# Transposes of tile 2's keys and queries by transfers instead of TensorE, with the work around them dealt anew

## The chip, the cores and the metric

The kernel runs on one core of one Trainium2 chip. A core has TensorE (PE; its weight loads are shown apart as PEld), VectorE (DVE), ScalarE (ACT), GpSimd (POOL) and SyncE (SP), and 16 DMA engines that serve the queues of all of them. The metric is the device time of one execution in microseconds.

## The reference

Windowed attention over q, k and v of shape (batch 8, heads 8, sequence 576, head size 64), then a two-layer network with a quick GELU over its 4608 rows of 512.

```python
# attention, window = 32
scores = scale * np.matmul(q, k.transpose(0, 1, 3, 2))
mask = np.abs(pos[:, None] - pos[None, :]) <= window
scores = np.where(mask, scores, -1000000000.0)
...
attn = attn / (np.sum(attn, axis=-1, keepdims=True) + 1e-09)
np.matmul(attn, v)
...
# x: (4608, 512), w_in: (512, 2048), w_out: (2048, 512)
h = x @ w_in
g = h * (1.0 / (1.0 + np.exp(-1.702 * h)))
return (g @ w_out).astype(np.float32)
```

## The kernel before

The 4608 rows are cut into 36 units of 128 and nine tiles of four units (512 rows); the rows of queries are shifted by 32 against those of keys. The order of all instructions is written out by hand. On each engine they run in that order, and each waits for the semaphores of what it needs.

**Attention of a unit.** `load_kq(c, u)` has GpSimd's queue bring the keys or queries of unit `u`, cast to bf16, into a staging buffer (`kst` or `qst`, five of each). They must be transposed, so that the head size lies on the partitions: `kT` and `qT`, seven buffers of each. `T_dma(c, u)` does that by a transposing transfer on SyncE's queue (L240); `turn(u)` is `T_dma("q", u)` and `T_dma("k", u + 1)`. `T_pe(which, eng)` does it on TensorE: three tensors at a time, four 128x128 transposes each, into PSUM (L249), and one copy each from PSUM by the engine named. `scores(u, tag)` multiplies keys and queries in 24 small products and takes the exponential on ScalarE (L284); it needs the queries of `u` and the keys of `u` and `u + 1`. `band(u)` masks on VectorE (L314), `values(u, tag)` multiplies with the values, `norm(u)` divides on VectorE (L344, L345). `x_T` and `x_T2` transpose the result for one or two units into `xT`. The values come by `load_v(u)` on GpSimd's queue, and GpSimd copies them to an odd offset with `odd_v(u)` (L227). `fetch(u)` is the loads of `q` of `u`, `k` of `u + 1` and `v` of `u + 1`; `ahead("kq", u)` leaves the values out.

**The two layers.** Both use a scheme of seven products on halves of the matrices in place of eight. It needs sums of weights (`w1_sums`, `w2_sums`), of inputs (`x_sums`) and of activations (`g_sums`; `g0_sum` for tile 0), all on VectorE. `l1_group(t, n, fill, side)` is a quarter of layer one of tile `t`: seven products into four PSUM banks, two copies on ScalarE and two additions on VectorE (L537, L543) between them, four GELUs on ScalarE (L524). Between its products, `fill(1)`, `fill(7)`, `fill(2)` and `fill(4)` put in pieces of layer two of the tile before, and `side(0)` and `side(1)` sums on VectorE. Layer two is one list of pieces, `l2`, of one product each; `do(l2, n)` issues the next `n`. Its first 32 pieces (`layer2_plain`) are one part of tile 0 without the scheme; the copies of the results out of PSUM go with certain pieces, on the engine that `l2eng` or `seed2` names at that point. Stores go on SyncE's queue.

**Where the change lies.** `opening` computes the attention of tiles 0 and 1 and layer one of tile 0. `first_layer1` is layer one of tile 1 with layer two of tile 0 between: four groups, `n` from 0 to 3. In each, two odd-offset copies and the loads `fetch(12 + n)` are issued on GpSimd. In groups 1 to 3, after product 7's fill, `T_pe` transposes the keys and queries of tile 2's units 8 to 11 (and 12's keys) on TensorE; in group 3, `turn(12)` and `turn(13)` send units 12 and 13 to SyncE. Then `run` computes the attention of units 8 to 15 with layer two between: units 8 to 11 are tile 2's, 12 to 15 tile 3's. From `back(2)`, layer one of tile 2, on, every tile goes the same way: `front` and `back`, with its transposes by `T_dma`.

Of the kernel before, what the change touches and what calls it, by code (L numbers as in the profile page):

```python
# [16 lines left out]
BF16 = mybir.dt.bfloat16  # L17
F16 = mybir.dt.float16
I32 = mybir.dt.int32
AF = mybir.ActivationFunctionType  # L20
ALU = mybir.AluOpType

SQ = 64
# [3 lines left out]
class _Kernel:  # L27
# [201 lines left out]


    def place(self, c, u):
        t = self.sb(c + "T", [128, 4, 128], BF16, 7)
        (self.kT if c == "k" else self.qT)[u] = t
        return t

    def T_dma(self, c, u):
# [1 line left out]
            return  # L238
        src = self.stage.pop((c, u))
        self.nc.sync.dma_start_transpose(self.place(c, u), src.rearrange("p h d -> p (h d)"))  # L240

    def T_pe(self, which, eng):

        tp = self.bank("t", [128, 4, 4, 128], BF16, "tp")
        which = [(x[0], int(x[1:])) for x in which]
        for i, (c, u) in enumerate(which):
            src = self.stage.pop((c, u)).rearrange("p h d -> p (h d)")
            for hp in range(4):
                self.nc.tensor.transpose(tp[:, i, hp, :], src[:, 128 * hp:128 * hp + 128], self.ident)  # L249
        for i, x in enumerate(which):  # L250
            self.copy(eng, self.place(*x), tp[:, i])

# [9 lines left out]
            self.sc.setdefault(u, []).append(x)  # L264
            self.mm(x, self.ident, self.bias, start=True)

    def scores(self, u, tag):
        kT, q = self.kT[u], self.qT[u]
        nxt = self.k_first if u == self.NU - 1 else self.kT[u + 1][:, :, 0:64]
        sc = self.score_banks(tag)  # L270
        for hp in range(4):
            c = 128 * hp
            start = hp == 0
            for eo in range(2):
                r = slice(64 * eo, 64 * eo + 64)
                lo, hi = sc[eo][0:64], sc[eo][64:128]
                self.mm(lo[:, c:c + 64], kT[r, hp, 0:64], q[r, hp, 0:64], start=start)
                self.mm(hi[:, c:c + 128], kT[r, hp, 64:128], q[r, hp, :], start=start)
                self.mm(lo[:, c + 64:c + 128], nxt[r, hp, :], q[r, hp, 64:128], start=False)
        if u % 2 == 0:  # L280
            self.pp = self.sb("p", [128, 2, 2, 8, SQ], BF16, 2)
        p = self.p[u] = self.pp[:, u % 2]
        for eo in range(2):
            self.nc.scalar.activation(p[:, eo].rearrange("k h s -> k (h s)"), sc[eo], AF.Exp, scale=self.scale)  # L284

    def scores_pair(self, u):

# [15 lines left out]
        for x in range(2):  # L303
            for eo in range(2):
                self.nc.scalar.activation(p[:, eo, x].rearrange("k h b s -> k (h b s)"), sc[2 * x + eo], AF.Exp,
                                          scale=self.scale)

    def band(self, u, eng=None):
        p = self.p[u]
        cross = [(2 * u + i) % 9 == 8 for i in range(2)]  # L310
        a, b = 0 if cross[0] else 1, 2 if cross[1] else 3
        pv = p.rearrange("p e (h b) s -> p (e h) b s", b=2)
        msk = self.mask[:, a:b + 1:b - a, :].rearrange("p (o b) s -> p o b s", o=1)
        (eng or self.nc.vector).tensor_mul(pv, pv, msk.to_broadcast([128, 8, 2, SQ]))  # L314

# [38 lines left out]
    def values_four(self, u):  # L354

        D = self.D
        p = [self.p.pop(u + i) for i in range(4)]
        b = {tag: self.bank(tag, name="pv") for tag in "AECt"}
        self.acc[u] = b | {"t0": b["t"][:, 0], "t1": b["t"][:, 1]}
        for tag in self.FOUR:  # L360
            lo, n, pad = self.four(tag)
            for i in range(n):
                x, h = divmod(lo + i, self.H)
                at, more = pad + i * (D + 1), pad * (i == 0)
                for blk in range(2):
                    vt = (self.ve[(u + x) % 9], self.odd(u + x))[blk].rearrange("p h d -> p (h d)")
                    self.mm(self.acc[u][tag][64 * blk:64 * blk + 64, at - more:at + D + 1],
                            p[x][:, h % 2, h // 2 * 2 + blk, :], vt[:, h * (D + 2) - more:h * (D + 2) + D + 1],
                            start=(i == 0))

    def norm_four(self, u, tags, units):
# [197 lines left out]
    def layer2_plain(self, t, pr):  # L569

        st = {}

        def part(i, f):
            if not st:
                st.update({j: self.bank("L" + "AB"[j], name="o") for j in range(2)})
                st["o"] = self.sb("o_sb", [128, 2, self.DM], F32, 2)
            lo = 256 * i + 128 * pr
            self.mm(st[i], self.g[t][:, f, lo:lo + 128], self.w2[:, f, :], start=(f == 0))
            if f == 15:
                self.copy((self.nc.vector, self.nc.scalar)[i * pr], st["o"][:, i, :], st[i])  # L580
                if i == 1:
                    self.store(t, pr, st["o"])

        return [lambda i=i, f=f: part(i, f) for q in range(8) for i in range(2) for f in (2 * q, 2 * q + 1)]
# [230 lines left out]
    @staticmethod  # L815
    def do(fs, n=99):
        for _ in range(min(n, len(fs))):
            fs.pop(0)()
# [76 lines left out]
    def run(self):  # L895
        pool, act = self.nc.gpsimd, self.nc.scalar
        self.l2eng = self.seed2 = act
        more = self.l2 = self.layer2_plain(0, 0) + self.layer2([(i, j) for i in range(self.NT) for j in range(2)][1:-1],
                                                               (self.NT - 1, 1))
        self.opening()  # L900
        self.do(self.x_sums(1))
        late = self.first_layer1()
        do = self.do
        dve = self.nc.vector
        self.scores(8, "t")
        self.scores(9, "AC")
        self.turn(14)
        self.turn(15)
        do(late)
        do(more, 20)  # L910
        self.scores(10, "BE")
        do(more, 12)
        self.l2eng = dve
        self.band(8)
        self.band(9)
        do(more, 4)
        self.values(8, "t")
        self.values(9, "AC")
        self.odd_v(12, pool)
        self.odd_v(13, pool)  # L920
        self.scores(11, "BE")
        self.norm(8)
        self.band(10)
        self.norm(9)
        do(more, 8)
        self.scores(12, "t")
        do(more, 4)
        self.values(10, "AC")
        self.norm(10)
        self.band(11)  # L930
        self.scores(13, "BE")
        do(more, 8)
        self.x_T2(8, "t", act)
        self.values(11, "AC")
        self.norm(11)
        self.scores(14, "BE")
        do(more, 4)
        self.x_T(10, "A", dve)
        do(more, 2)
        self.x_T(11, "C", dve)  # L940
        self.scores(15, "t")
        do(more, 2)
        do(self.x_sums(2))
        self.seed2 = dve
        self.odd_v(14, pool)
        self.odd_v(15, pool)
        self.ahead("kq", 16)
        late = self.back(2)
        for t in range(3, self.NT):
            self.front(t, late)  # L950
            late = self.back(t)
        self.l2eng = act
        self.do(late, 2)
        self.do(self.l2, 16)
        self.do(late)
        self.do(self.l2, 999)

    def first_layer1(self):

        def b(*which):  # L960
            return [lambda i=i, j=j: self.w2_sums((i,), j) for i, j in which]

        dv = b((3, 0), (3, 1), (1, 0), (1, 1))
        extra = {0: [lambda: self.w1_sums((4,), 1), lambda: self.g0_sum(1)] + b((2, 0), (2, 1)), 1: b((4, 0), (4, 1)),
                 2: [lambda: self.g0_sum(2)], 3: []}
        for n in range(4):
            if n == 3:
                self.turn(12)
                self.turn(13)
            self.odd_v(8 + n, self.nc.gpsimd)  # L970
            self.fetch(12 + n)

            def fill(i):
                self.do(self.l2, dict(zip((1, 7, 2, 4), ((1, 1, 3, 3), (1, 1, 3, 5), (2, 2, 8, 4), (2, 2, 6, 6))[n]))[i])
                self.do(dv, {1: 2, 7: 1, 2: 0, 4: 2}[i] if n else {1: 0, 7: 1, 2: 0, 4: 1}[i])
                if i == 7 and n:
                    self.T_pe([("k8", "q8", "k9"), ("q9", "k10", "q10"), ("k11", "q11", "k12")][n - 1], self.nc.scalar)

            self.l1_group(1, n, fill, lambda i: self.do(dv, 1))
            dv += self.g_sums(1, 2 * n, 2) + extra[n]  # L980
        return dv

# [45 lines left out]
```

## Time and profile before

| | us |
|---|---|
| median of 3 runs (279.33 to 280.86) | 279.39 |
| the profiled execution | 279.59 |
| its span | 277.8 |
| layer one of tile 1 begins (first product after 43) | 43.47 |
| first scores of unit 8 | 65.31 |
| last scores ahead of tile 2's layer one (unit 15) | 77.78 |
| layer one of tile 2 begins | 78.39 |

Times inside the execution count from the start of the span. The profile is of one execution. A row of the timeline gives start and length in us, the engine, the line, the operation, out<-in by the program's names, the shape, and how many were merged; in brackets, idle time before it and what ended it. The names are `sc` for scores, `pv` for values, `tp` for transposes in PSUM, `h` for layer one, `o` for layer two, `g` and `gs` for activations and their sums, `a` and `b` for sums of weights. Matmuls are pipelined, so the length of a row is longer than its share of the time; the spacing of starts is the measure. A row of DMA issues ends with the time from issue to landing. SPq is SyncE's queue.

### The profile page before, as it was taken

Reading aid. Unit: us, or ns where it says so; the run is one execution under the profiler, and the core shown is the slowest. Engines: PE = TensorE matmul, PEld = TensorE weight load, DVE = VectorE, ACT = ScalarE, POOL = GpSimd, SP = SyncE. Lnnn points to the kernel's source line nnn. Section 1 sums busy time; section 2 is a strip of 40 time slices with the busy share of each in tenths; the row PEclk is TensorE's granted clock in tenths of the full one; section 3 lists DMA queues with packets and bytes.
Section 4 is the critical chain, followed back from the end, with each engine's and each line's share of the span. In section 5 each row is a group of like instructions: output and inputs, shape, how many; then the busy total and the mean of one; then the engine's idle time right before and its main releaser. Section 6 shows DMA issues by size and latency. Waiting matters only on the chain.

```text
span 277.8 us, 8904 instructions
## 1 busy us (share of the span) xinstructions
PE 266.3 (96%) x3652; PEld 224.8 (81%) x3652; DVE 212.1 (76%) x487; ACT 197.3 (71%) x346; POOL 138.6 (50%) x216
## 2 busy tenths in 40 slices
PE   1989999999999999999999999999999999999994
PEld 1668656888888888888888888888888888888883
DVE  3455898897899788878888887888798878855631
ACT  2586896989896689568966895698569856577420
POOL 8895597999592089729641974294430000000000
PEclk9999999999999999999999999999999999999999
DMA  8999999999999999999999999999992024202033
GB/s 86 166 206 195 178 207 168 170 150 164 139 162 189 155 121 153 174 176 166 188 178 153 130 172 148 163 145 139 136 136 77 2 82 74 76 2 76 2 113 117
DMA packets 150809, 37.74 MB, mean 136 GB/s; under 512 B 138608, under 2 KB 146416, under 8 KB 150768
## 3 DMA queue, kind: packets, MB, share of 16 engines
q0 software_dynamic: 106656, 18.42, 96.4%
q1 hardware_dynamic: 43664, 18.23, 38.0%
q8 instruction: 28, 0.46, 0.7%
q10 hardware_dynamic: 448, 0.52, 0.6%
q14 instruction: 13, 0.11, 0.1%
HBM read 36.83 MB, written 9.44 MB: 167 GB/s over the span
## 4 chain that ended last, share of the span: by engine, by line
PE 91%; DVE 4%; ACT 2%; issue 1%; POOL 1%; POOLq 0%; DVEq 0%
PE o L70 40%; PE h L70 39%; PE sc L70 5%; PE pv L70 4%; PE tp L179 1%; PE tp L203 1%; POOL kq L154 1%; ACT p L284 1%; DVE xn L345 1%; PE tp L409 0%; PE tp L249 0%; DVE b L433 0%; DVE o_sb L67 0%; PE tp L397 0%; ACT kq L67 0%
## 5 line engine op out<-in xcount | busy, mean ns | idle before, releaser
L524 ACT ACTIVATE g<-h 128x512 f16<-128x512 f32 x128 | 72.2, 599 | 37.9 <-PE h L70 31.6
L70 PEld LDWEIGHTS <-g 128*128 128x128 f16 x568 | 54.6, 98 | 8.1
L70 PE MATMUL h<-xs,a 128*128 128x256 f16 x384 | 57.6, 272 | 0.3 <-DVE h L537 0.3
L70 PEld LDWEIGHTS <-a 128*128 128x128 f16 x512 | 49.7, 97 | 8.8 <-issue 0.6
L70 PEld LDWEIGHTS <-w 128*128 128x128 f16 x496 | 47.6, 98 | 7.7
L70 PE MATMUL h<-xT,w 128*128 128x256 f16 (+1 forms) x368 | 53.6, 277 | 0.1
L70 PE MATMUL o<-w,g 128*128 128x256 f16 (+1 forms) x304 | 49.8, 284 | 0.0
L70 PEld LDWEIGHTS <-gs 128*128 128x128 f16 x416 | 39.7, 98 | 5.5 <-issue 0.2
L227 POOL COPY vo<-ve 64x264 int32<-64x264 int32 x71 | 35.1, 494 | 16.4 <-DMA ve<-in_v_dram 10.0
L70 PE MATMUL o<-b,gs 128*128 128x256 f16 x280 | 43.3, 273 | 0.0
L70 PE MATMUL o<-b,g 128*128 128x256 f16 x264 | 38.5, 273 | 0.0
L213 POOL DMA_DIRECT2D ve<-in_v_dram x40 | 34.1, 860 | 5.4 <-DMA w<-in_moe_w_out_dram 1.8
L537 DVE TENSOR_TENSOR h<-h,s 128x512 f32<-128x512 f32 x32 | 22.3, 698 | 18.3 <-PE h L70 18.2
L284 ACT ACTIVATE p<-sc 128x512 bf16<-128x512 f32 x64 | 32.6, 619 | 1.1 <-PE sc L70 1.0
L143 POOL DMA_DIRECT2D qst<-in_q_dram x35 | 28.2, 807 | 1.7 <-issue 1.6
L543 DVE TENSOR_TENSOR h<-h,s 128x512 f32<-128x512 f32 x32 | 22.3, 698 | 7.6 <-PE h L70 7.4
L143 POOL DMA_DIRECT2D kst<-in_k_dram x31 | 26.4, 854 | 0.6 <-DMA qst<-in_q_dram 0.4
L67 ACT COPY h<-h 128x512 f32<-128x512 f32 x32 | 18.8, 589 | 10.4 <-PE h L70 9.8
L886 POOL COPY seen<-gs 1x1 f16<-1x1 f16 x17 | 3.3, 196 | 39.3 <-DVE gs L456 39.3
L314 DVE TENSOR_TENSOR p<-p,mask 128x1024 bf16<-128x1024 bf16 x32 | 21.8, 699 | 0.7 <-ACT p L284 0.7
L67 ACT COPY o_sb<-o 128x256 f32<-128x256 f32 (+1 forms) x24 | 11.1, 462 | 12.8 <-PE o L70 12.8
L67 ACT COPY s<-h 128x512 f32<-128x512 f32 x32 | 19.2, 600 | 0.8
(94 smaller groups left out, 377.8 us busy)
## 6 DMA issues: line engine op xcount, KB each, us to landing
out_dram<-o_sb SPq DMA_DIRECT2D x33, 256.0 KB, 3.8
ve<-in_v_dram POOLq DMA_DIRECT2D x32, 128.0 KB, 6.3
kst<-in_k_dram POOLq DMA_DIRECT2D x25, 128.0 KB, 6.0
qst<-in_q_dram POOLq DMA_DIRECT2D x21, 128.0 KB, 5.7
w<-in_moe_w_out_dram POOLq DMA_DIRECT2D x4, 512.0 KB, 11.1
w<-in_moe_w_in_dram POOLq DMA_DIRECT2D x3, 512.0 KB, 9.3
qst<-in_q_dram POOLq DMA_DIRECT2D x7, 96.0 KB, 6.0
kq<-in_q_dram POOLq DMA_DIRECT2D x2, 256.0 KB, 6.0
```

The lines of the kernel that those rows point to most:

```text
L67: (eng.copy if eng is self.nc.scalar else eng.tensor_copy)(out, in_)
L70: self.nc.tensor.matmul(out, lhsT, rhs, start=start, stop=stop, skip_group_check=True)
L143: self.nc.gpsimd.dma_start(t[off:off + n], src[b, :, s:s + n, :].rearrange("h s d -> s h d"))
L154: self.nc.gpsimd.dma_start(self.stage["first"][0:n // j, :, at:at + j], src[0, :, lo:lo + n, :].rearrange("h (p j) d -> p h j d", j=j))
L213: self.nc.gpsimd.dma_start(t[off:off + n, :, :self.D], self.v[b, :, s:s + n, :].rearrange("h s d -> s h d"))
L227: eng.tensor_copy(*((words(vo[64:128]), words(self.ve[u % 9][64:128])), (words(vo[0:64]), words(nxt)))[i])
L284: self.nc.scalar.activation(p[:, eo].rearrange("k h s -> k (h s)"), sc[eo], AF.Exp, scale=self.scale)
L314: (eng or self.nc.vector).tensor_mul(pv, pv, msk.to_broadcast([128, 8, 2, SQ]))
L524: act.activation(g[:, f, 256 * half:256 * half + 256], bank.rearrange("p (i n) -> p i n", i=2), AF.Gelu_apprx_sigmoid)
L537: dve.tensor_add(e, b, s7)
L543: dve.tensor_add(c, b, s7)
L886: self.nc.gpsimd.tensor_copy(self.seen, self.gs[t - (n == 0)][0:1, 2, c, 255:256])
```

## The change

- `T_pe` is gone. In `first_layer1` the nine tensors that it transposed are issued by `T_dma` on SyncE's queue, three in each of groups 0 to 2; group 3 issues those of units 12 and 13, as before.
- The values of units 14 to 16 are loaded in group 3, after the keys and queries; before, one each in groups 1 to 3.
- The numbers of layer-two pieces and of sums in each gap of the four groups are new (`chunks`, `sums`): 56 pieces in place of 50. `w1_sums((4,), 1)` comes after the sums of group 0.
- The queries of units 12 and 13 lie side by side in one buffer, and their scores are one run of 40 products (`scores_two`). Scores of unit 10 come right behind those of 8 and 9, the second of its exponentials held back. Units 10 and 11 are transposed together by `x_T2`.
- `layer2_plain` copies both results on ScalarE, and `l2eng` is ScalarE in place of VectorE between units 8 and 15.

TensorE's order from layer one of tile 2 on is the same in both.

```diff
     def place(self, c, u):
+        if c == "q" and u in (12, 13):
+            if u % 2 == 0:
+                self.qT[u] = self.sb("q_two", [128, 4, 256], BF16, 1)
+            return self.qT[u - u % 2][:, :, 128 * (u % 2):128 * (u % 2) + 128]
...
-    def T_pe(self, which, eng):
-
-        tp = self.bank("t", [128, 4, 4, 128], BF16, "tp")
-        which = [(x[0], int(x[1:])) for x in which]
-        for i, (c, u) in enumerate(which):
-            src = self.stage.pop((c, u)).rearrange("p h d -> p (h d)")
-            for hp in range(4):
-                self.nc.tensor.transpose(tp[:, i, hp, :], src[:, 128 * hp:128 * hp + 128], self.ident)
-        for i, x in enumerate(which):
-            self.copy(eng, self.place(*x), tp[:, i])
...
+    def scores_two(self, u, tags):
+
+        k, q = [self.kT[u + i] for i in range(3)], self.qT[u]
+        sc = [x for tag in tags for x in self.score_banks(tag)]
+        for hp in range(4):
+            c = 256 * (hp % 2)
+            for eo in range(2):
+                r = slice(64 * eo, 64 * eo + 64)
+                for i in range(5):
+                    lo, hi = max(0, 64 * (i - 1)), min(256, 64 * (i + 1))
+                    rows = slice(64 * (i % 2), 64 * (i % 2) + 64)
+                    self.mm(sc[2 * (hp // 2) + eo][rows, c + lo:c + hi], k[i // 2][r, hp, rows], q[r, hp, lo:hi],
+                            start=c == 0 and i < 2)
...
             if f == 15:
-                self.copy((self.nc.vector, self.nc.scalar)[i * pr], st["o"][:, i, :], st[i])
+                self.copy(self.nc.scalar, st["o"][:, i, :], st[i])
...
         dve = self.nc.vector
+        do(more, 3)
         self.scores(8, "t")
         self.scores(9, "AC")
+        exps = self.scores(10, "BE", True)
         self.turn(14)
         self.turn(15)
         do(late)
-        do(more, 20)
-        self.scores(10, "BE")
-        do(more, 12)
-        self.l2eng = dve
+        do(more, 3)
         self.band(8)
         self.band(9)
-        do(more, 4)
+        self.l2eng = act
+        do(more, 16)
+        do(exps)
+        do(more, 8)
         self.values(8, "t")
         self.values(9, "AC")
...
-        do(more, 8)
-        self.scores(12, "t")
-        do(more, 4)
+        do(more, 12)
+        self.scores_two(12, ("t", "BE"))
         self.values(10, "AC")
+        self.band(11)
         self.norm(10)
-        self.band(11)
-        self.scores(13, "BE")
...
-        do(more, 4)
-        self.x_T(10, "A", dve)
-        do(more, 2)
-        self.x_T(11, "C", dve)
+        do(more, 6)
+        self.x_T2(10, "A", dve)
...
-        extra = {0: [lambda: self.w1_sums((4,), 1), lambda: self.g0_sum(1)] + b((2, 0), (2, 1)), 1: b((4, 0), (4, 1)),
+        extra = {0: [lambda: self.g0_sum(1)] + b((2, 0), (2, 1)) + [lambda: self.w1_sums((4,), 1)], 1: b((4, 0), (4, 1)),
                  2: [lambda: self.g0_sum(2)], 3: []}
         for n in range(4):
-            if n == 3:
-                self.turn(12)
-                self.turn(13)
+            for c, u in ((("k", 8), ("q", 8), ("k", 9)), (("q", 9), ("k", 10), ("q", 10)),
+                         (("k", 11), ("q", 11), ("k", 12)), (("q", 12), ("k", 13), ("q", 13), ("k", 14)))[n]:
+                self.T_dma(c, u)
             self.odd_v(8 + n, self.nc.gpsimd)
-            self.fetch(12 + n)
+            self.ahead("kq", 12 + n)
+            for u in ((13,), (), (), (14, 15, 16))[n]:
+                self.load_v(u)
+
+            chunks = ((1, 2, 3, 3), (2, 2, 5, 4), (4, 4, 5, 4), (4, 4, 5, 4))[n]
+            sums = ((0, 0, 1, 1, 2), (2, 1, 1, 1, 2), (2, 1, 1, 1, 1), (2, 1, 1, 1, 1))[n]
...
-                self.do(self.l2, dict(zip((1, 7, 2, 4), ((1, 1, 3, 3), (1, 1, 3, 5), (2, 2, 8, 4), (2, 2, 6, 6))[n]))[i])
-                self.do(dv, {1: 2, 7: 1, 2: 0, 4: 2}[i] if n else {1: 0, 7: 1, 2: 0, 4: 1}[i])
-                if i == 7 and n:
-                    self.T_pe([("k8", "q8", "k9"), ("q9", "k10", "q10"), ("k11", "q11", "k12")][n - 1], self.nc.scalar)
+                at = (1, 7, 2, 4).index(i)
+                self.do(self.l2, chunks[at])
+                self.do(dv, {1: sums[0], 7: sums[1], 2: 0, 4: sums[4]}[i])
...
-            self.l1_group(1, n, fill, lambda i: self.do(dv, 1))
+            self.l1_group(1, n, fill, lambda i: self.do(dv, sums[2 + i]))
```

More of the change, by code (lines that the diff above doesn't have):

```diff
@@ L265, in seed, with scores @@
             self.mm(x, self.ident, self.bias, start=True)
-    def scores(self, u, tag):
+    def scores(self, u, tag, hold=False):
         kT, q = self.kT[u], self.qT[u]
@@ L282, in scores @@
         p = self.p[u] = self.pp[:, u % 2]
-        for eo in range(2):
-            self.nc.scalar.activation(p[:, eo].rearrange("k h s -> k (h s)"), sc[eo], AF.Exp, scale=self.scale)
+        exps = [lambda eo=eo: self.nc.scalar.activation(p[:, eo].rearrange("k h s -> k (h s)"), sc[eo], AF.Exp,
+                                                         scale=self.scale) for eo in range(2)]
+        self.do(exps, 1 if hold else 2)
+        return exps
     def scores_pair(self, u):
@@ L306, in scores_pair @@
                                           scale=self.scale)
+    def scores_two(self, u, tags):
[10 more added lines that the diff above has]
+                            start=c == 0 and i < 2)
+        self.pp = self.sb("p", [128, 2, 2, 8, SQ], BF16, 2)
+        p = self.pp.rearrange("k e x (y b) s -> k e x y b s", y=2)
+        for i in range(2):
+            self.p[u + i] = p[:, :, :, :, 2 * i:2 * i + 2, :]
+        for x in range(2):
+            for eo in range(2):
+                self.nc.scalar.activation(p[:, eo, x].rearrange("k y b s -> k (y b s)"), sc[2 * x + eo], AF.Exp,
+                                          scale=self.scale)
     def band(self, u, eng=None):
@@ L311, in band @@
         a, b = 0 if cross[0] else 1, 2 if cross[1] else 3
-        pv = p.rearrange("p e (h b) s -> p (e h) b s", b=2)
+        pv = (p.rearrange("p e (h b) s -> p (e h) b s", b=2) if len(p.shape) == 4 else
+              p.rearrange("p e x y b s -> p (e x y) b s"))
         msk = self.mask[:, a:b + 1:b - a, :].rearrange("p (o b) s -> p o b s", o=1)
@@ L367, in values_four @@
                     self.mm(self.acc[u][tag][64 * blk:64 * blk + 64, at - more:at + D + 1],
-                            p[x][:, h % 2, h // 2 * 2 + blk, :], vt[:, h * (D + 2) - more:h * (D + 2) + D + 1],
+                            p[x][:, h % 2, h // 2 * 2 + blk, :] if len(p[x].shape) == 4 else
+                            p[x][:, h % 2, h // 4, h // 2 % 2, blk, :], vt[:, h * (D + 2) - more:h * (D + 2) + D + 1],
                             start=(i == 0))
@@ L943, in run @@
         do(self.x_sums(2))
-        self.seed2 = dve
+        self.seed2 = self.l2eng = dve
         self.odd_v(14, pool)
```

## The prediction

> **What bounds the kernel now.** I read the page first, its busy slices and its chain, then the busy time by stretches, then the timeline of TensorE.
>
> ```profile
> span 277.8 us, 8904 instructions
> PE   1989999999999999999999999999999999999994
> PE 91%; DVE 4%; ACT 2%; issue 1%; POOL 1%; POOLq 0%; DVEq 0%
> ```
> ```profile
> 57.00:65.00 8.00, 7.75 (x78) 6.78 (x76) 7.18 (x15) 6.99 (x16) 7.76 (x12) 1.00 1.77 138
> 65.00:72.00 7.00, 7.00 (x172) 5.75 (x170) 4.39 (x11) 6.94 (x14) 5.03 (x8) 1.00 2.19 151
> 72.00:80.00 8.00, 8.00 (x184) 6.49 (x183) 7.49 (x24) 6.66 (x13) 6.83 (x11) 1.00 1.34 162
> ```
>
> TensorE is full from the second slice to the last and carries 91% of the chain, so whatever is taken from its queue counts. The columns of the stretches are length, busy time of PE, PEld, DVE, ACT and POOL, granted clock, DMA share and GB/s. In the stretches that the change touches (tile 1's layer one and the switch to tile 2) TensorE idles only 0.25 us, and the clock is granted in full. But a DMA share above 1 says that several packets per DMA engine are under way all the time. The change takes work from the first resource and gives it to the second.
>
> From the start of tile 2's layer one the order of both kernels is the same on TensorE, and TensorE is full from there nearly to the end. So I work out when that layer starts, and the shift carries over to the end one to one. The profiled execution took 279.59 us (span 277.8 and 1.8 around it); the median of the runs is 279.39, 0.2 less.
>
> **The transposes leave TensorE.** Three groups of twelve go.
>
> ```profile
> 49.62 0.39 PE L249 MATMUL tp<-ident,kst 128*128 128x128 bf16 x4
> 50.30 0.60 PE L70 MATMUL h<-xs,a 128*128 128x256 f16 x4
> 50.73 0.60 PE L70 MATMUL h<-xT,w 128*128 128x256 f16 x4
> 56.63 1.04 PE L70 MATMUL o<-b,gs 128*128 128x256 f16 x8
> 57.92 0.60 PE L70 MATMUL h<-xs,a 128*128 128x256 f16 x4 [0.25 <-DVE h L537]
> ```
>
> A group runs from 49.62 to 50.30, 0.68 us; three give 2.0 us. On ScalarE nine copies go; it is not last there. Four products of 256 columns take 0.43 us (50.30 to 50.73), so one takes 0.11, and the eight at 56.63 should end at 57.50; the next starts at 57.92. That 0.4 us is TensorE waiting for VectorE's sum, which stands behind `w2_sums` and `g_sums`.
>
> **Sums and copies dealt anew.** Two plain results move from VectorE to ScalarE, `w1_sums(4)` and two `w2_sums` move later, and six more layer-two products stand in tile 1. I take the 0.4 us as gained: VectorE loses 2 x 0.68 us and its sums are spread. At worst the same wait appears in another group, 0. The nine copies that leave ScalarE cover the two that come.
>
> ```profile
> 51.94 0.68 DVE L67 COPY o_sb<-o 128x512 f32<-128x512 f32 x1
> 50.98 0.59 ACT L67 COPY qT<-tp 128x512 bf16<-128x512 bf16 x1
> 66.19 1.28 ACT L284 ACT_TABLE_LOAD   x1
> 67.49 3.05 ACT L284 ACTIVATE p<-sc 128x512 bf16<-128x512 f32 x6
> ```
>
> One new wait: the table load and the exponentials of units 8 and 9 keep their distance to the end of tile 1's products (1.28 us and four times 0.51), while 27 layer-two products stand ahead of `values(8)` and `values(9)` where 36 stood before. Nine at 0.11 is 1 us of cover less; by the rows the masked unit 9 comes about 0.3 us after TensorE asks for it. I charge 0.3.
>
> **Score runs joined.**
>
> ```profile
> 67.40 1.04 PE L70 MATMUL o<-w,g 128*128 128x256 f16 x8
> 68.37 0.45 PE L70 MATMUL sc<-qT,kT 64*64 64x64 bf16 x24
> 68.74 1.05 PE L70 MATMUL o<-w,gs 128*128 128x256 f16 x8
> 99.59 0.70 PE L70 MATMUL sc<-qT,kT 64*64 64x64 bf16 x48
> 100.22 0.61 PE L70 MATMUL o<-w,g 128*128 128x256 f16 x4
> ```
>
> A run of 24 costs 0.37 us (68.37 to 68.74) and some 0.10 at its entry (67.40 and eight times 0.11 is 68.27); one of 48 costs 0.63 and the entry. So joining two runs saves 2 x 0.47 less 0.73, 0.2 us. Unit 10 joins 8 and 9, and 12 joins 13: 0.4 us. In 40 instructions for 48 the pair may gain or lose 0.1.
>
> Were nothing else late, tile 2 would start 2.0 + 0.4 + 0.4 - 0.3 = 2.5 us earlier, 2.9 if the 0.3 is not paid.
>
> **Nine more transfers.** This is the term that decides, and it is priced in DMA time. The rows are the DMA queues' packets, MB and share, in the stretches 48 to 54, 64 to 69.5 (two rows), 54 to 58 (two), 46 to 72.7 (two), and 46 to 59. q0 carries the loads, q1 the transposes and stores of SyncE.
>
> ```profile
> q0 software_dynamic: 7266, 0.92, 239.8%
> q0 software_dynamic: 4348, 0.55, 174.4%
> q1 hardware_dynamic: 1498, 0.36, 42.7%
> q0 software_dynamic: 3026, 0.38, 149.7%
> q1 hardware_dynamic: 266, 0.49, 32.9%
> q0 software_dynamic: 23240, 2.92, 181.5%
> q1 hardware_dynamic: 3133, 1.21, 27.0%
> q1 hardware_dynamic: 281, 0.51, 10.6%
> ```
>
> From 48 to 54 loads run alone and without a break: 0.92 MB in 6 us, 6.5 us per MB, 0.85 us for a load of 128 KB (0.131 MB). From 64 to 69.5 loads take 0.55 x 6.5 = 3.6 us of 5.5, which leaves 1.9 us for 0.36 MB of transposes: 0.70 us for one of 128 KB, if nothing idled. That is the upper bound; the lower is nothing, if transposes slip between the loads' packets. I take 0.60, near the row. Stores come out the same way at (4 - 2.5) / 0.49, 3.1 us per MB.
>
> Now the budget up to 72.7, when the load of unit 16's keys lands:
>
> ```profile
> 66.47 0.88 POOL L143 DMA_DIRECT2D kst<-in_k_dram  x1 [0.19 <-issue]
> kst<-in_k_dram POOLq DMA_DIRECT2D x1, 128.0 KB, 6.2
> 64.16 1.19 SPq L240 DMA_TRANSPOSE kT<-kst  x1
> kT<-kst SPq DMA_TRANSPOSE x1, 5.2
> 72.83 1.19 SPq L240 DMA_TRANSPOSE kT<-kst  x1
> kT<-kst SPq DMA_TRANSPOSE x1, 3.6
> 59.69 0.90 POOL L213 DMA_DIRECT2D ve<-in_v_dram  x1
> 77.78 0.45 PE L70 MATMUL sc<-qT,kT 64*64 64x64 bf16 x24
> 78.39 0.60 PE L70 MATMUL h<-xT,w 128*128 128x256 f16 x4
> ```
>
> Between 46 and 72.7 loads take 2.92 x 6.5 = 19.0 us, stores 0.51 x 3.1 = 1.6, transposes (1.21 - 0.51) x 5.3 = 3.7: 24.3 of 26.7 us, so 2.4 us are free. The nine transposes add 9 x 0.60 = 5.4. The values of units 14 and 15 (the first issued at 59.69, ahead of unit 14's queries) now stand behind unit 16's keys in GpSimd's queue: 1.7 us less. The load lands 5.4 - 1.7 - 2.4 = 1.3 us later, at 74.0. Its transpose took 3.6 us, when GpSimd had no load left to send; with the values of 14 to 16 behind it I take 4.4, between 3.6 and the 5.2 of the one at 64.16, which had such loads beside it. The keys are there at 78.4. `scores(15)` needs them; it started at 77.78, and tile 2's first product at 78.39, 0.61 later, which stays. So tile 2 starts 0.6 us later, not 2.5 earlier: the gain on TensorE turns into waits at `scores_two(12)`, which needs unit 14's keys, and at units 14 and 15. The forecast is 279.59 + 0.6 - 0.2 = 280.0 us. With 0.70 and 5.2 it is 0.9 + 0.8 more, 281.7; with 0.50 and 3.6 it is 1.7 less, 278.3.
>
> The earlier transposes are covered: `scores(8)` comes at about 63.5, 17 us after the first loads landed. SyncE's queue holds tile 0's stores behind `q10`; units 11 and 12 wait behind them for ScalarE's copy, at about 52.5, when those loads are still under way: nothing. The odd-offset copies on GpSimd that need the values of 14 to 16 hold up tile 3's first loads by some 2 us; these are used after 99.59.
>
> [...]
>
> **Rivals.** *The transfers are hidden* (0.25): transposes cost the loads nothing, and the last keys come when they came before or sooner. Then 2.9 us are gained, 276.7, or 276.5 on the scale of the median. For it: the shares above 1 show packets overlapping. Against: in two stretches of different mix the prices above fill the time. *TensorE goes cold* (0.15), slower: unit 14's keys landed at 69.4 (64.16 and 5.2). Nine transposes less the 1.8 us or so that are free until then, and nothing yet saved by the values, make it about 3.6 later, 73.0; TensorE without waits asks at about 70.3. That is one idle stretch of 2.7 us.
>
> ```profile
> 7.40 1.03 PE L70 MATMUL sc<-bias,ident 128*128 128x512 bf16 x2
> 13.03 1.15 PE L70 MATMUL sc<-bias,ident 128*128 128x512 bf16 x4
> 39.98 0.60 PE L70 MATMUL o<-w,g 128*128 128x512 f16 x2
> ```
>
> At the opening, after idling, two products of 512 columns take 1.03 us; at 13.03 four take 1.15, at 39.98 two take 0.60. So the array runs at about half rate up to some point between 7.4 and 13.0. [...] Against it: the gap is split over three waits, and the clock column stays at 1.00. [...]
>
> **How the numbers follow.** The forecast's case has 0.60, its own range 278.3 to 281.7. The range of 276.3 to 281.9 takes in the hidden case and leaves out the cold one. One per cent, about what a measurement here can tell from no change, is 2.8 us: below 276.6 or above 282.2. Half of the hidden case lies below: 0.14 with a little of the first; the cold case and the first one's tail lie above: 0.15; 0.71 within.
>
> **What would show it.** Right: no `tp<-ident,kst` on TensorE between 49 and 62; the chain of waits enters transposes between 68 and 79; TensorE idles 2 to 4 us in all before `scores_two`, `scores(14)` and `scores(15)`; loads issued after 46 land later than 5.2 us. Wrong: tile 2's first product below 77, or loads that keep their 5.2 us beside the new transposes; or products of 512 columns at 0.43 us spacing after a wait.

## The result and the profile after

The changed kernel takes 286.69 us, the median of six runs (286.43 to 287.66); the kernel before, beside it, 279.64 (279.25 to 281.6). The ratio is 1.0246, with a 95% interval of 1.0209 to 1.0282: slower, by 7 us. The forecast was 280.0 in a range of 276.3 to 281.9. It was wrong, so were its rivals, and the time lies 4.8 us above the upper end of the range.

First the page of the changed kernel: TensorE's busy time and granted clock in 40 slices, and the chain of work that ended last.

```profile
PE   1979999998199999999999999999999999999995
PEclk9999999999759999999999999999999999999999
PE 72%; DMA 18%; POOL 4%; issue 2%; DVE 2%; SPq 1%; ACT 0%; POOLq 0%; DVEq 0%
```

One slice of 7.1 us is nearly empty, the clock drops at the same place, and TensorE carries 72% of the chain, not 91%. Next the stretches (columns as before: length, busy time of PE, PEld, DVE, ACT and POOL, granted clock, DMA share, GB/s), then TensorE's timeline, reduced to the scores and to the first product of tile 2's layer one.

```profile
72.00:80.00 8.00, 1.80 (x50) 1.50 (x51) 1.35 (x3) 0.56 (x2) 4.04 (x8) 0.67 1.95 164
80.00:85.00 5.00, 5.00 (x77) 3.84 (x72) 2.24 (x8) 3.53 (x8) 3.39 (x6) 0.50 1.02 201
```
```profile
65.91 0.44 PE L70 MATMUL sc<-qT,kT 64*64 64x64 bf16 x22 [1.07 <-DMA kT<-kst]
...
72.69 0.24 PE L70 MATMUL sc<-q_two,kT 64*64 64x64 bf16 x2 [0.86 <-DMA q_two<-qst]
76.41 0.32 PE L70 MATMUL sc<-q_two,kT 64*64 64x128 bf16 x2 [3.48 <-DMA q_two<-qst]
78.76 1.07 PE L70 MATMUL sc<-q_two,kT 64*64 64x64 bf16 x36 [2.03 <-DMA kT<-kst]
...
85.75 0.45 PE L70 MATMUL sc<-qT,kT 64*64 64x64 bf16 x24
...
86.61 0.60 PE L70 MATMUL h<-xT,w 128*128 128x256 f16 x4
```

Tile 2 begins at 86.61 instead of 78.39, 8.2 us later. The profiled execution is 287.53 us (span 285.6), 7.9 above the one before. So the whole loss is made ahead of tile 2. TensorE waits 7.4 us there, always for transposes; the last wait, for the keys of unit 14, is over at 78.76. From 72 to 80 it is busy for 1.80 us of 8, where the kernel before had no gap. And from 80 to 85, where TensorE has work again, the clock column reads 0.50.

Now the transfers. The first fence is the DMA queues from 46 to 72.7 us, the stretch of the prediction's budget: all packets, then loads (q0) and SyncE's transposes and stores (q1). The second is the row of all packets of the kernel before in the same stretch. The third is 53 to 60 of the changed kernel, where q1 holds transposes alone.

```profile
DMA packets 23252, 4.08 MB, mean 153 GB/s; under 512 B 22993, under 2 KB 22993, under 8 KB 23249
q0 software_dynamic: 17510, 2.20, 157.1%
q1 hardware_dynamic: 5739, 1.84, 50.0%
```
```profile
DMA packets 26376, 4.18 MB, mean 156 GB/s; under 512 B 26117, under 2 KB 26117, under 8 KB 26373
```
```profile
DMA packets 6791, 1.08 MB, mean 155 GB/s; under 512 B 6791, under 2 KB 6791, under 8 KB 6791
q0 software_dynamic: 4816, 0.61, 136.8%
q1 hardware_dynamic: 1975, 0.47, 54.0%
```

Read the two totals together: 4.18 MB before, 4.08 after. With nine more transposes to do, the DMA engines moved no more than without them. The transposes put 0.63 MB more through q1, and the loads lost 0.72 MB.

What that did to the tensors shows in SyncE's queue. L240 of the kernel before is L244 here; the transpose of unit 14's keys goes out when their load has landed, so its start tells when that was: issued at 58.81 before and 62.83 here, the load landed 5.3 and 8.8 us later, at 64.1 and 71.6, and the transposes go out at 64.16 and 71.79. The rows are those of unit 14 and, last, unit 16. The second fence is the DMA view of the same two, with the time from issue to landing.

```profile
71.79 1.22 SPq L244 DMA_TRANSPOSE kT<-kst  x1
...
75.83 1.24 SPq L244 DMA_TRANSPOSE qT<-qst  x1
77.18 1.53 SPq L244 DMA_TRANSPOSE kT<-kst  x1
```
```profile
kT<-kst SPq DMA_TRANSPOSE x1, 6.9
...
kT<-kst SPq DMA_TRANSPOSE x1, 5.5
```

Unit 14's keys are sent to be transposed at 71.79; before, at 64.16. They land 6.9 us later, at 78.7, not at 69.4. Unit 16's go out at 77.18 (before 72.83), some 0.6 us of it because SyncE is still issuing the transpose ahead of them, and land at 82.7.

### The profile page after: what moved, and what is told of

Read it like the earlier page. It is cut to its first block, busy times and chain, and to the rows that moved or that the text cites. A ratio compares the mean times of both kernels' runs of the same rounds, so it can differ in the third digit from the quotient of the medians.

```text
span 285.6 us, 8822 instructions
## 1 busy us (share of the span) xinstructions
PE 266.2 (93%) x3608; PEld 223.9 (78%) x3608; DVE 210.5 (74%) x483; ACT 194.1 (68%) x340; POOL 138.1 (48%) x216
## 4 chain that ended last, share of the span: by engine, by line
PE 72%; DMA 18%; POOL 4%; issue 2%; DVE 2%; SPq 1%; ACT 0%; POOLq 0%; DVEq 0%
PE o L70 34%; PE h L70 31%; DMA w<-in_moe_w_out_dram 5%; DMA w<-in_moe_w_in_dram 4%; PE sc L70 4%; DMA qst<-in_q_dram 3%; DMA ve<-in_v_dram 3%; PE pv L70 3%; DMA kT<-kst 2%; POOL vo L227 1%; PE tp L179 1%; POOL o_sb L192 1%; SPq L244 1%; POOL kq L154 1%; POOL qst L143 0%
## 5 line engine op out<-in xcount | busy, mean ns | idle before, releaser
L70 PEld LDWEIGHTS <-g 128*128 128x128 f16 x568 | 55.2, 99 | 8.5
L70 PE MATMUL o<-b,g 128*128 128x256 f16 x264 | 39.5, 277 | 0.0
L276 ACT ACTIVATE p<-sc 128x512 bf16<-128x512 f32 x60 | 30.5, 621 | 1.3 <-PE sc L70 1.1
L67 ACT COPY o_sb<-o 128x256 f32<-128x256 f32 (+1 forms) x27 | 12.6, 465 | 12.9 <-PE o L70 12.9
```

Of the source, the lines that this page charges most:

```text
L67: (eng.copy if eng is self.nc.scalar else eng.tensor_copy)(out, in_)
L70: self.nc.tensor.matmul(out, lhsT, rhs, start=start, stop=stop, skip_group_check=True)
L276: exps = [lambda eo=eo: self.nc.scalar.activation(p[:, eo].rearrange("k h s -> k (h s)"), sc[eo], AF.Exp, scale=self.scale) for eo in rang ...
```

## The experiments

**The nine transfers alone.** The kernel before with `T_dma` for the nine tensors, and nothing else of the change.

```diff
-            if n == 3:
-                self.turn(12)
-                self.turn(13)
+            for c, u in ((("k", 8), ("q", 8), ("k", 9)), (("q", 9), ("k", 10), ("q", 10)),
+                         (("k", 11), ("q", 11), ("k", 12)), (("q", 12), ("k", 13), ("q", 13), ("k", 14)))[n]:
+                self.T_dma(c, u)
...
-                if i == 7 and n:
-                    self.T_pe([("k8", "q8", "k9"), ("q9", "k10", "q10"), ("k11", "q11", "k12")][n - 1], self.nc.scalar)
```

> The kernel of before with nothing changed but the nine transposes, which go to SyncE's queue as in the changed kernel. Queue theory: each of the nine costs the loads as much DMA time as a load does, 0.85 us, so that unit 14's keys land about 7.5 us late, at 71.5, and the time is 285 to 287.5, all of the change's loss. Rival (a good part of the loss is the new order around them): 281 to 284.

Measured: 286.46 us (285.89 to 286.81), ratio 1.0247, interval 1.0229 to 1.0266. This one part has the whole loss. Unit 14's keys are sent at 71.72, as in the changed kernel. In its timeline the scores of unit 13, which need them, wait as long, and tile 2 starts at 85.34:

```profile
78.32 0.64 PE L70 MATMUL sc<-qT,kT 64*64 64x64 bf16 x22 [1.18 <-DMA kT<-kst]
...
85.34 0.60 PE L70 MATMUL h<-xT,w 128*128 128x256 f16 x4
```

**Nine transposes that nobody waits for.** The kernel before keeps its transposes on TensorE, and SyncE sends the same nine tensors through a transfer as well, into a buffer that nobody reads. That tells the load on the DMA engines from the changed order on TensorE.

```diff
+            for x in ((("k", 8), ("q", 8), ("k", 9)), (("q", 9), ("k", 10), ("q", 10)), (("k", 11), ("q", 11), ("k", 12)), ())[n]:
+                self.nc.sync.dma_start_transpose(self.sb("spare", [128, 4, 128], BF16, 7),
+                                                 self.stage[x].rearrange("p h d -> p (h d)"))
```

> The kernel of before, its nine transposes still on TensorE, with nine more transposing transfers of the same staged tensors into buffers that nothing reads. TensorE waits for none of them. Queue theory (they delay the loads): unit 14's keys land at 70 to 72 in place of 64.15 and the time rises by 4 to 8 us. Rival (the harm is in waiting for the nine themselves): below 281 us.

One run: 286.34 us, beside a median of 279.73 for the kernel before. In its timeline unit 13's scores wait for unit 14's keys until about the same moment, and tile 2 starts at 85.49:

```profile
78.88 0.64 PE L70 MATMUL sc<-qT,kT 64*64 64x64 bf16 x22 [2.19 <-DMA kT<-kst]
...
85.49 0.60 PE L70 MATMUL h<-xT,w 128*128 128x256 f16 x4
```

So nothing needs to depend on the nine transfers for them to cost some 7 us. They cost it by what they do to the other transfers: the load of unit 14's keys, issued at 64.76, landed 6.9 us later, at 71.7, against 64.1 in the kernel before.

**Less other traffic.** The changed kernel without the loads of the values of units 9 to 16. It leaves out that part of the input: those units are computed with old values in the buffers.

```diff
-            for u in ((13,), (), (), (14, 15, 16))[n]:
-                self.load_v(u)
...
-            self.fetch(u)
+            self.ahead("kq", u)
```

> The changed kernel without the loads of the values of units 9 to 16, so that later units use old values: eight loads less, at 0.85 us 6.8 us of DMA time, about what nine transposes add. Queue theory: unit 14's keys are transposed by 70 to 71, TensorE waits less than 1 us ahead of the joined scores of units 12 and 13, the clock stays at 1.00, and the time is 276.5 to 278. Rival (the transposes are late by their own latency and by SyncE's order, whatever the loads do): the waits stay, 283 us or more.

One run: 278.51 us, beside 279.73, at a clock of 1.000. It is the only kernel here that is faster than the one before, and it does less. The timeline of TensorE shows one short wait for a transpose in place of 7.4 us, and its waits between 50 and 92 us are these (in total, times, longest):

```profile
72.53 0.66 PE L70 MATMUL sc<-q_two,kT 64*64 64x64 bf16 x36 [0.51 <-DMA kT<-kst]
...
77.73 0.60 PE L70 MATMUL h<-xT,w 128*128 128x256 f16 x4
```
```profile
PE sc L70 <- DMA kT<-kst: 0.5, 1, 0.5
PE h L70 <- DVE h L556: 0.5, 1, 0.5
PE o L70 <- DVE o_sb L642: 0.4, 1, 0.4
```

Take away about as many bytes as the transposes add and the loss is gone, although the nine transfers and SyncE's order stay. With the run before it, that leaves traffic as the cause. How much of it is the DMA engines' time and how much that loads wait for earlier loads in GpSimd's queue, these two runs don't separate. The time lies 0.5 us above what was expected, and the rows say why it isn't lower. Tile 2 starts 0.66 us earlier than before, and TensorE still waits 0.9 us for VectorE, twice. Where transfers don't hold TensorE up, VectorE does next.

**The rest of the change.** The changed kernel with `T_pe` and its calls put back as they were before:

```diff
+    def T_pe(self, which, eng):
...
-            for c, u in ((("k", 8), ("q", 8), ("k", 9)), (("q", 9), ("k", 10), ("q", 10)),
-                         (("k", 11), ("q", 11), ("k", 12)), (("q", 12), ("k", 13), ("q", 13), ("k", 14)))[n]:
-                self.T_dma(c, u)
+            if n == 3:
+                self.turn(12)
+                self.turn(13)
```

> The changed kernel with the nine transposes back on TensorE, all the rest as changed (new order, joined score runs, copies on ScalarE, values of units 14 to 16 loaded late). Queue theory (the nine transposing transfers slow the loads, and TensorE then waits and goes cold): unit 14's keys are transposed by about 69 as before the change, tile 2's layer one begins 0.4 to 0.9 us earlier than the 78.39 of before, 278.6 to 279.2 us in all, clock 1.00. Rival (the rest of the change costs the time): 283 us or more.

281.55 us (280.4 to 283.02), ratio 1.0064, interval 1.0043 to 1.0085: a miss, and slower than the kernel before. GpSimd's timeline offered a cause. A load of queries waited for a transpose to free its staging buffer:

```profile
63.49 0.88 POOL L143 DMA_DIRECT2D qst<-in_q_dram  x1 [2.40 <-DMA q_two<-qst]
```

So the next kernel has a sixth staging buffer, and the one after it the values at their old place as well:

```diff
-        t = self.stage[c, u] = self.sb(c + "st", [128, self.H, self.D], BF16, 5)
+        t = self.stage[c, u] = self.sb(c + "st", [128, self.H, self.D], BF16, 6)
```

> The kernel of e1_pe_transposes (transposes on TensorE, the rest as changed) with six staging buffers each for keys and queries in place of five. In e1 the queries of unit 14 were given the buffer of unit 12's, and GpSimd stood 2.4 us until their transposing transfer had landed; with six that wait is gone. If it was the cause of e1's 0.6 per cent, the load of unit 16's keys is issued at about 65 and the time is 278 to 279. If the late values (units 14 to 16 behind the keys) are, it stays at 280.5 to 282.

```diff
-            self.ahead("kq", 12 + n)
-            for u in ((13,), (), (), (14, 15, 16))[n]:
-                self.load_v(u)
+            self.fetch(12 + n)
```

> The same with the values of units 14 to 16 loaded one in each of groups 1 to 3, as before the change. What is left of the change is the new deal of pieces, sums and copies and the joined score runs. By the prediction's sums (0.4 us of VectorE's wait and 0.4 us of joined runs gained, 0.3 paid): 278.7 to 279.6. Rival (these edits cost time by themselves): 280.5 or more.

The sixth buffer changes nothing: 281.42 us (280.53 to 282.05), ratio 1.0067, interval 1.004 to 1.0093. That wait was no cause. The values do: at their old place it is 279.54 (279.33 to 280.26), ratio 1.0008, interval 0.9999 to 1.0018. Here are the timelines of TensorE, first with late values, then with early ones.

```profile
77.67 0.44 PE L70 MATMUL sc<-qT,kT 64*64 64x64 bf16 x22 [1.50 <-DMA kT<-kst]
...
80.10 0.60 PE L70 MATMUL h<-xT,w 128*128 128x256 f16 x4
```
```profile
68.54 1.03 PE L70 MATMUL o<-w,gs 128*128 128x256 f16 x8 [0.25 <-DVE o_sb L653]
...
73.09 0.68 PE L70 MATMUL sc<-q_two,kT 64*64 64x64 bf16 x40
...
75.88 0.45 PE L70 MATMUL sc<-qT,kT 64*64 64x64 bf16 x24
...
78.31 0.60 PE L70 MATMUL h<-xT,w 128*128 128x256 f16 x4
```

Late values cost 1.9 us. In the profiled run unit 14's scores wait 1.50 us for the transpose of unit 15's keys. It was sent at 68.09, behind the late values (issued from 66.19 on), and took 9.5 us. With early ones it was sent between 67.85 and 68.0, and unit 14's scores run at 75.88 without a wait. The transpose of the next keys, unit 16's, took 5.5 us with late values and 4.0 with early ones. The first fence is the DMA view of unit 15's keys with late values, the second that of unit 16's, late and early:

```profile
kT<-kst SPq DMA_TRANSPOSE x1, 9.5
```
```profile
kT<-kst SPq DMA_TRANSPOSE x1, 5.5
...
kT<-kst SPq DMA_TRANSPOSE x1, 4.0
```

That wait isn't the whole of it. With five buffers and late values the profiled run has no such wait, tile 2 starts at 79.20, and it still takes 281.89 us. With early values there is no wait for a transfer, and the rest of the change is worth nothing that a measurement shows.

**Three transfers of nine.** The last kernel, with the first three tensors (`k8`, `q8`, `k9`) by transfer and six on TensorE.

```diff
+            if n == 0:
+                for c, u in (("k", 8), ("q", 8), ("k", 9)):
+                    self.T_dma(c, u)
...
-                if i == 7 and n:
+                if i == 7 and n > 1:
```

> The kernel of e56 with the first three transposes (unit 8's keys and queries, unit 9's keys) by transfers and six on TensorE. Queue theory at 0.85 us each: the loads fall 2.6 us behind, unit 14's keys are transposed by 71.5 to 72, before TensorE asks for them, and 0.5 to 0.7 us of TensorE are gained over e56. Rival (any transfer more delays the last keys at once): 1 to 2.5 us slower than e56.

283.49 us (281.71 to 284.64), ratio 1.0137, interval 1.0096 to 1.0179: a third of the transfers lost about 4 us, not a third of 7 and more than either expectation had, and the runs spread over 3 us. The timeline of TensorE and three stretches of the profiled run:

```profile
77.49 0.24 PE L70 MATMUL sc<-qT,kT 64*64 64x64 bf16 x2 [1.40 <-DMA qT<-qst]
77.98 0.49 PE L70 MATMUL sc<-qT,kT 64*64 64x64 bf16 x22 [0.24 <-DMA kT<-kst]
...
81.63 0.61 PE L70 MATMUL h<-xT,w 128*128 128x256 f16 x4
```
```profile
77.00:78.00 1.00, 0.27 (x6) 0.13 (x6) 0.20 (x1) 0.00 (x0) 1.00 (x2) 1.00 1.09 224
78.00:79.00 1.00, 1.00 (x25) 0.77 (x26) 0.00 (x0) 0.56 (x2) 1.00 (x3) 0.61 0.93 122
79.00:80.00 1.00, 1.00 (x9) 0.80 (x7) 0.00 (x0) 0.53 (x2) 1.00 (x2) 0.50 1.44 257
```

Tile 2 starts 3.3 us later than without the three. Some 2.1 of it is there at unit 14's scores (77.98 against 75.88 without them). The other 1.2 comes between those and tile 2, which take 3.65 us instead of 2.43, while the clock is at half. That split holds for this run alone: the fastest and the slowest of the four both had a full mean clock, so where the spread comes from stays open.

**What the half clock costs.** The changed kernel, with products ahead of the joined scores that keep TensorE busy and that nobody reads: first 64 of them, then 46.

```diff
+        warm = self.bank("A", name="warm")
+        for i in range(64):
+            self.mm(warm[:, 0:256], self.w1[:, 0, 0:128], self.w2[:, 0, 0:256], start=True)
```

> The changed kernel with 64 products of 256 columns (64 x 0.11 = 7.0 us) into a free PSUM bank ahead of the joined scores of units 12 and 13; their result is not used. They fill the wait from 71.7 to 78.8 without shortening it. Cold theory (half the clock after the idle stretch costs time): the clock stays at 1.00, the work from the joined scores to tile 2's layer one takes 5 to 5.5 us in place of 7.85, and the time falls by 2 to 3 us to about 284. Rival (the low clock costs nothing, since the next keys are late anyway): 286 to 287.5.

> The changed kernel with 46 filler products of 256 columns (5.1 us) in front of the joined scores, where 64 (7.2 us) stood before; their results are read by nobody. In the run with 64 the filler ended at 79.11 and unit 14's keys had landed at 78.25, so the filler itself held the scores up by about 0.9 us. With 46 it ends at about 77.1, ahead of the keys, and the idle time that is left is about 1 to 1.5 us. If the half clock costs what the changed kernel's trace suggests (7.85 us from the joined scores to tile 2, against 5.2 us in the version with TensorE transposes), the time falls by 1.5 to 2.7 us against the changed kernel, to 284.0 to 285.2, at a clock of 0.998 or more. Rival: the keys and queries of units 15 and 16, which land up to 82.8, set the start of tile 2 anyway; then it stays within 0.7 us of the changed kernel, 286.0 to 287.0, as with 64.

> The changed kernel as it is, on the same chip as the run with 46 fillers, so that the two can be compared: 286.4 to 287.2 us, clock 0.982 to 0.988, tile 2's first product at 86 to 87.

With 64: 286.4 us (285.96 to 289.94), ratio 1.0272, interval 1.0198 to 1.0346. With 46: 286.22 (285.48 to 287.6), 1.0244, interval 1.0217 to 1.0272. The changed kernel again on the chip of the latter: 286.25 (283.77 to 287.14), 1.0226, interval 1.0189 to 1.0262. The clock was 0.994 or more with fillers, so they do what they should, and the times agree within their spread. Here are the timelines with 46 fillers and of the changed kernel beside it.

```profile
79.00 0.66 PE L70 MATMUL sc<-q_two,kT 64*64 64x64 bf16 x36 [2.02 <-DMA kT<-kst]
...
84.21 0.60 PE L70 MATMUL h<-xT,w 128*128 128x256 f16 x4
...
111.66 0.61 PE L70 MATMUL h<-xs,a 128*128 128x256 f16 x4 [0.47 <-DVE xs L460]
```
```profile
78.21 1.06 PE L70 MATMUL sc<-q_two,kT 64*64 64x64 bf16 x36 [2.47 <-DMA kT<-kst]
...
85.65 0.60 PE L70 MATMUL h<-xT,w 128*128 128x256 f16 x4
```

From the joined scores to tile 2 it is 5.2 us at full clock and 7.4 with much of it at half; so the half clock does take 2.2 us of that stretch. But in this pair the keys came 0.8 us later with the fillers, and 0.5 us went back to VectorE at 111.66. The two profiled runs differ by 0.7 us (285.9 and 286.6); the medians show no gain, and an estimate from the two intervals leaves room for at most 0.8 us of one. Both expectations were partly wrong: the cost in the stretch is real, and removing it bought little or nothing. Why the whole of it doesn't come back, with spreads of 2 to 3 us between runs, is open.

## Why the prediction was wrong, point by point

- **The bound.** The budget saw the right resource: transposes collide with loads (155 GB/s with both from 53 to 60, 154 with loads alone from 48 to 54 before), and the 2 us that TensorE saves become waits. The bound of the kernel moved to transfers, as it said.
- **The price of a transposing transfer was the term that was mis-sized.** The prediction took 0.60 us and held 0.70 for the upper bound. In the stretch 53 to 60 of the changed kernel, by the prediction's own method, loads take 0.61 x 6.5 = 4.0 of 7 us and 0.47 MB of transposes the other 3.0: 6.4 us per MB, 0.84 us for 0.131 MB. That is a load's price, 0.85. The rows behind the 0.70 were no bound: in those 5.5 us 0.91 MB moved, 165 GB/s, more than loads alone reach (154), so the mix there was cheaper than the one that the change makes. Nine cost 7.6 us, where 5.4 stood. The transposes that were there already the budget priced higher, at 5.3 us per MB or 0.70 each.
- **The free time didn't reach unit 14.** Of 2.4 free us, about 1.8 were to be used up by unit 14. Its keys were sent to the transpose 7.6 us later than before (71.79 and 64.16), which is nine times 0.84 with nothing taken off. One reason shows on GpSimd: the load of these keys waits for a load of values, which it doesn't need (this row is GpSimd's timeline in the changed kernel):

```profile
62.83 0.89 POOL L143 DMA_DIRECT2D kst<-in_k_dram  x1 [1.57 <-DMA ve<-in_v_dram]
```

  The load waited for is the eighth before it, counting a load issued in two halves twice; whether the number in flight is limited, no run tested. So here one load that landed late held the next one back, with GpSimd idle for 1.57 us.
- **For unit 16's keys the budget held, once the price is right.** At 6.4 us per MB the transposes already there take 4.5 us, and 1.6 are free, not 2.4. With transfers alone the load of unit 16's keys should then land 7.6 - 1.6 = 6.0 us later than before, and in the changed kernel, less the 1.7 of the late values, 4.3. The rows are its issue and its DMA view, first with transfers alone, then in the changed kernel:

```profile
72.25 0.89 POOL L143 DMA_DIRECT2D kst<-in_k_dram  x1
kst<-in_k_dram POOLq DMA_DIRECT2D x1, 128.0 KB, 6.5
```
```profile
70.51 0.88 POOL L143 DMA_DIRECT2D kst<-in_k_dram  x1
kst<-in_k_dram POOLq DMA_DIRECT2D x1, 128.0 KB, 6.0
```

  It landed at 78.75 and at 76.51, against 72.67 before: 6.1 and 3.8 us later. So the sum holds there; it was worked out for a tensor that didn't decide.
- **The late values had a cost that was booked too low.** For unit 16's keys they did about what the prediction said: 2.2 us earlier than with transfers alone, where 1.7 stood, though those two kernels differ in the other edits too. But on the kernel with TensorE's transposes late values cost 1.9, where only 0.8 stood for a slower last transpose (4.4 in place of 3.6). Among the nine transfers they make no difference that shows in the time: the transfers alone, with early values, take 286.46, the whole change 286.69.
- **The last link was the wrong one.** The forecast hung tile 2 on unit 16's keys, with 2 to 4 us of waits ahead; there were 7.4. The joined scores of units 12 and 13, which need unit 14's, set it: most of them run at 78.76, against 73.09 where nothing is late, 5.7 us; the 5.2 us from there to tile 2 took 7.85 at half clock, 2.6 more. Together that is 8.3 us against that kernel, 8.2 against the kernel before. Unit 16's keys, at 82.7, came 3 us before their scores.
- **The earlier transposes** were put at nothing. The scores of unit 10, drawn ahead by the change, waited 1.07 us at 65.91 for unit 11's keys, which had been sent behind the stores at 56.64 and were 9.2 us under way. It didn't count in the end, since the joined scores waited longer anyway.
- **The cold rival** named the right mechanism, at 0.15: its one wait of 2.7 us became 6.4 us of waits at the joined scores, and the clock fell to half (0.50 from 75 to 84). How long an idle stretch it takes for that, and so what the rival would cost, was the author's estimate, and no run shows such a limit. In its place the runs show a fall to half within a wait of 3.48 us (the changed kernel) and one after waits of 1.40 and 0.24 (three transfers), 1.00 kept through one of 1.50, and 2.6 us more in the changed kernel's stretch from the joined scores to tile 2. The lateness that the rival stood on (3.6 us, against 9.3 for unit 14's keys) was too small by more than half, and with fillers the half clock is gone and the medians are no lower. The hidden rival was refuted outright.
- **TensorE's gain.** The transposes left TensorE, as forecast. Without values, tile 2 came 0.66 us early with 1.4 us of waits still in it, so without waits it would have come some 2.1 us early, against the 2.5 forecast. Nearly half of that met VectorE, which the prediction had relieved by 0.4. With transposes on TensorE, 0.5 us were forecast for sums, copies and joined runs; tile 2 started 0.08 us earlier, with a new wait for VectorE of 0.25 at 68.54, and the medians show none.

## What to carry to other kernels

Where the DMA engines are full, price a new transfer by its bytes at the rate that the full queues show for its kind (here, by the author's estimates, 6.4 us per MB for a transpose, 6.5 for a load and 3.1 for a store), and take off free time only where the trace shows that the next transfers could have been issued into it. Then look for the first consumer that runs dry, not the last tensor. Here 2.0 us of work moved from a full engine to full queues took 7.6 us of their time and cost 7, because what it delayed stood in front of everything else.

## What the runs showed of the hardware

In the two stretches that the prices come from, transposes beside loads left the throughput as it was with loads alone. From 48 to 54 in the kernel before, loads alone moved 0.92 MB in 6 us (154 GB/s); the changed kernel made 155 GB/s from 53 to 60 with loads and transposes together. Other stretches were faster: 165 GB/s by loads and transposes from 64 to 69.5 in the kernel before, and 221 with stores from 54 to 58. Within a microsecond of the changed kernel (58 to 59) the two queues moved about as many packets each:

```profile
q0 software_dynamic: 427, 0.05, 81.0%
q1 hardware_dynamic: 415, 0.11, 79.2%
```

In that microsecond the loads had half of the packets (427 of 842) and about a third of the bytes (0.05 of 0.16 MB). From 64 to 65 the packets are shared the same way (371 and 366), but from 53 to 60 as a whole the loads had 4816 of 6791. How the DMA engines choose between the two queues, no run tested.

The clock fell to half without one long idle stretch. With three transfers, waits of 1.40 and 0.24 us came before it: the columns show 1.00 from 77 to 78, 0.61 between 78 and 79 and 0.50 from 79 to 81, and from 77 to 78 TensorE still worked for 0.27 us. With late values, six buffers and TensorE's transposes one wait of 1.50 us left it at 1.00. So the longest wait alone doesn't tell these two runs apart; what does, no run tested. In the changed kernel, with waits of 0.86, 3.48 and 2.03 us (over at 72.69, 76.41 and 78.76), the column reads 1.00 up to 74, 0.87 from 74 to 75, 0.50 from 75 to 84, 0.51 from 84 to 85, and 1.00 again from 85 on.
